# The first half of k over the hardware queues: a fused attention and feed-forward kernel

## The chip, the cores and the metric

The kernel runs on one core of a Trainium2 chip. The metric is the device time of one execution in microseconds (us). The core has five engines that run side by side, each taking its own instructions in order: TensorE (PE in the profile; PEld is its weight load), VectorE (DVE), ScalarE (ACT), GpSimd (POOL) and SyncE (SP). Transfers between the device's memory and the core's memory go through 16 DMA engines. They are issued on queues: GpSimd's is a software queue (q0 in the profile) whose transfers may change the number type on the way; SyncE's (q1) and ScalarE's (q10) are hardware queues, on which this kernel moves data in its own type.

## The reference

q, k and v have the shape [8, 8, 576, 64] (batch, heads, sequence, head size), all float32. Attention runs in a window of 32 positions to each side; its result is put together over the heads and goes through two matrix products with a smooth unit between them. The constants are filled in here:

```python
scores = matmul(q, k.transpose(0, 1, 3, 2)) / sqrt(64)
scores = where(abs(pos[:, None] - pos[None, :]) <= 32, scores, -1e9)
attn = softmax(scores)                       # over the last axis
x = matmul(attn, v).transpose(0, 2, 1, 3).reshape(4608, 512)
h = x @ w_in                                 # [4608, 2048]
g = where(h >= 1, h, where(h <= -1, 0, (h + 1) ** 2 / 4))
out = g @ w_out                              # [4608, 512]
```

## The kernel before

The matrix work is done in bfloat16, with sums in float32. The tokens are taken in blocks of 256 (`TB`); a block's first product is made in eight steps of 256 columns (L504, into the tile `hp`), each followed by the unit on ScalarE and VectorE (`rr`, `mx`, `gT`, L508 to L516), and the second product (L433, L444, L460) follows in pieces laid between later steps. The loop at L482 counts these steps as `a`. The attention of the eight batches is cut into pieces (scores, sums) that a hand-written table places at steps of that loop. All engines follow the order in which the program writes their instructions (`manual_schedule`); nothing is reordered.

The loop can't begin before the first block of attention is there, so the kernel opens with a stage of its own, which is where the change lies. Four heads of a batch lie in one half of the partitions and four in the other. The first batch's q and k come in two halves of heads, and each half in two transfers (`load_half`, L80; `h` picks the half of the partitions that is read from). In the first half:

- q is loaded in float32 into `q32` by SyncE (h = 0) and ScalarE (h = 1), 128 rows of 2304 B each. It is turned into bfloat16 on chip by `cast` (L338): VectorE converts five of nine parts of each row (`cut` = 5), ScalarE the other four, into `qb`.
- k is loaded by GpSimd's software queue in two transfers that convert to bfloat16 on the way, into `kh`. They are GpSimd's first two DMA issues. Behind them on GpSimd stand an `affine_select` (L131, from which VectorE makes the identity and the band masks), four loads of v (L134), four pieces of w_in, and then the second half of q and k and more weights (L149 to L157).

Q and k are then transposed on TensorE by `tpose` (L169), which writes into PSUM in two parts, of five and four column groups. Where its source is a tile that `cast` made, it transposes 128x128 at once (L189, nine matmuls for q). Where its source came straight from a transfer, it takes the two 64-column halves one after the other (L187, eighteen matmuls). The two parts are copied out of PSUM into `qT` and `kT` (L190), the first by ScalarE and the second by VectorE.

The order of the opening (L346 to L370) is: eleven filler matmuls on TensorE that use no input (`keep_warm`, L336, tile `z`), the cast of q, q's transposes, q's two copies, k's transposes, three fillers, k's two copies, then the first scores. Scores begin with matmuls that put the band mask into PSUM (L206), then the products of kT and qT (L227), then the exponential on ScalarE (L235, tile `pt`). After more fillers come the sums over v and over ones (L293), logarithm and exponential on ScalarE for the reciprocal (L299, L300), and the scaled result into `xT` on VectorE (L305). The first `hp` reads that `xT`.

Of the kernel before, what the change touches and what calls it, by code (L numbers as in the profile page):

```python
# [7 lines left out]
FP = mybir.dt.float32  # L8
# [6 lines left out]
def kernel(  # L15
# [19 lines left out]
    nc = tc.nc  # L35
    B, H, S, D = q.shape
# [40 lines left out]
    qn, kn, vn = {}, {}, {}  # L77
    HD = (slice(0, 64), slice(64, 128))

    def load_half(half, t, h, eng=None, x=None):  # L80

        src, dst, nm = ((q, qn, "qh"), (k, kn, "kh"))[t]
        if (0, half) not in dst:
            dst[0, half] = early.tile([128, 2, S], BF, name=nm, tag=nm, bufs=2) if x is None else x
        (eng or nc.gpsimd).dma_start(out=dst[0, half][:, h], in_=src[0].rearrange(
            "(h y) (l p j) d -> h l p y (j d)", h=2, l=2, p=32)[h][half])
# [29 lines left out]
                            in_=moe_w_out.rearrange("(ko ki) f -> ki ko f", ki=128)[:, k0:k1, 256 * c:256 * c + 256])  # L116

    early = ctx.enter_context(tc.tile_pool(name="early", bufs=1))
    q32 = early.tile([128, 2, S], FP, name="q32")
    for h in range(2):  # L120
        load_half(0, 0, h, (nc.sync, nc.scalar)[h], q32)
    for h in range(2):
        load_half(0, 1, h)
    A.preload_act_table_set("natural_log_exp_and_others")
    warm = const.tile([128, 512], BF, name="warm")
    V.memset(warm, 0.0)
# [35 lines left out]
    def qkT(b, t):  # L162
        if t == 0:
            return qTs[b % 3][:, PAD:]
        if b not in kT:
            kT[b] = ktp.tile([128, NY * S], BF, name="kT")
        return kT[b]

    def tpose(b, n, t, copy, ps):  # L169


        half, part = divmod(n, 2)
        j0, j1 = ((0, 5), (5, 9))[part]
        if b:
            src = qn[b] if t == 0 else kn[b]
            src = [src[:, half + 2 * h] for h in range(2)]
            dst = qkT(b, t).rearrange("d (y e p j) -> d y e p j", y=2, e=2, j=9)[:, half, :, :, j0:j1]
            like = "d j (e p) -> d e p j"
        else:
            src = (qn, kn)[t][b, half]  # L180
            src = src if src.shape[1] == 9 else [src[:, h] for h in range(2)]
            dst = qkT(b, t).rearrange("d (y l p j) -> d l y p j", l=2, p=32, j=9)[:, half, :, :, j0:j1]
            like = "d j (p y) -> d y p j"
        for j in range(j0, j1):
            if isinstance(src, list):
                for h in range(2):
                    nc.tensor.transpose(ps[HD[h], j - j0], src[h][:, D * j:D * j + D], ident)  # L187
            else:
                nc.tensor.transpose(ps[:, j - j0], src[:, j], ident)  # L189
        return lambda: copy(dst, ps[:, :j1 - j0].rearrange(like, p=64 if b else 32))  # L190
# [20 lines left out]
    def scores(b, ys, pars, cs, eng, pool=ps_s, w=128):  # L211

        if b not in pt:
            pt[b] = ptp.tile([128, 2, 2, 2, 512], BF, name="pt")
        ps = two_banks(pool)
        n = 0
        if eng is None:
            cols = (ys[1] - ys[0]) * (pars[1] - pars[0]) * (cs[1] - cs[0])
            add_mask([ps[:, h] for h in range(2)], cols, w)
        for y1 in range(*ys):  # L220
            for par in range(*pars):
                for c2 in range(*cs):
                    c = 2 * c2 + par
                    for a in range(2):
                        for h in range(2):
                            s0 = S * (y1 + 2 * a) + 64 * c
                            nc.tensor.matmul(ps[HD[a], h, w * n:w * n + w], kT[b][HD[h], s0:s0 + 64],  # L227
                                             qTs[b % 3][HD[h], PAD + s0 - 32:PAD + s0 - 32 + w],
                                             start=eng is not None, stop=True, skip_group_check=True)
                    n += 1  # L230
        p = pt[b][:, :, ys[0]:ys[1], pars[0]:pars[1], 128 * cs[0]:128 * cs[1] - 128 + w]
        m = 2 if n > cs[1] - cs[0] else 1
        p = p[:, :, ys[0] - ys[0]] if ys[1] - ys[0] == 1 else p[:, :, :, 0]
        like = "p h (y j) -> p h y j"
        A.activation(p, ps[:, :, :w * n].rearrange(like, y=m), AF.Exp, scale=D ** -0.5)  # L235
        mask(eng, p, mask4[:, :256 * n].rearrange("p (h j) -> p h j", h=2).rearrange(like, y=m))
# [81 lines left out]
    def tp1(pool):  # L318
        if pool is ps_h:
            return pool.tile([128, 8, 128], BF, name="tp", tag="hp")  # L320
        return pool.tile([128, 2, 8, 128], BF, name="tp", tag="bb")[:, 0]
# [10 lines left out]
    def keep_warm(n, pool, tag):  # L332

        z = pool.tile([128, 512], FP, name="z", tag=tag)
        for _ in range(n):
            nc.tensor.matmul(z, warm[:, :128], warm, start=True, stop=True)  # L336

    def cast(x, nm, cut):  # L338

        y = early.tile([128, 9, 2, D], BF, name=nm)  # L340
        o, i = y.rearrange("p j h d -> p h j d"), x.rearrange("p h (j d) -> p h j d", d=D)
        V.tensor_copy(o[:, :, :cut], i[:, :, :cut])
        A.copy(o[:, :, cut:], i[:, :, cut:])
        return y.rearrange("p j h d -> p j (h d)")

    with tc.tile_pool(name="ps_p", bufs=1, space=bass.MemoryType.PSUM) as ps_p:  # L346
        keep_warm(11, ps_h, "hp")

        V.memset(qkT(0, 0).rearrange("d (y s) -> d y s", y=NY)[:, :, S // 2:352], 0.0)
        for b in range(LONG):  # L350
            V.memset(qkT(b, 0).rearrange("d (y s) -> d y s", y=NY)[:, :, S - PAD:], 0.0)
        V.memset(qkT(0, 1).rearrange("d (y s) -> d y s", y=NY)[:, :, S // 2:320], 0.0)
        qn[0, 0] = cast(q32, "qb", 5)
        qq = [tpose(0, n, 0, (A.copy, V.tensor_copy)[n], tp1(ps_h)) for n in range(2)]
        for x in qq:
            x()
        kk = [tpose(0, n, 1, (A.copy, V.tensor_copy)[n], tp1((ps_n, ps_p)[n])) for n in range(2)]
        keep_warm(3, ps_h, "hp")
        for x in kk:
            x()  # L360
        scores(0, (0, 1), (0, 2), (0, 2), None)
        scores(0, (0, 2), (0, 1), (2, 3), None, ps_n, 32)
        scores(0, (1, 2), (0, 2), (0, 2), None, ps_p)
        keep_warm(4, ps_h, "hp")
        e0 = sums(0, 0, 0, TB)
        keep_warm(2, ps_h, "hp")
        e1 = sums(0, 1, 0, TB, ps_p)
        keep_warm(7, ps_h, "hp")
        e0()
        e1()  # L370
# [111 lines left out]
    for a in range(NF * NB + NF):  # L482
        t, f = divmod(a, NF)
# [70 lines left out]
```

## Time and profile before

| what | value |
| --- | --- |
| time, median of 4 runs | 308.59 us (308.56 to 308.73) |
| the profiled execution: time | 308.56 us |
| its span, first to last instruction | 306.8 us |
| TensorE busy | 300.4 us (98% of the span) |
| VectorE busy | 241.8 us (79%) |
| ScalarE busy | 192.3 us (63%) |
| GpSimd busy | 76.8 us (25%) |
| granted TensorE clock | 1.00 throughout |
| first q issues, SyncE and ScalarE | 0.74 us, 4.4 and 3.8 us to landing |
| first k issues, GpSimd | from 1.26 us, 1.26 us for both |
| first v issues, GpSimd | from 2.94 us, 3.44 us for the four |
| first scores on TensorE | 8.62 us |
| first exponential on ScalarE | 9.08 us |
| first xT on VectorE | 12.57 us |

The times in the lower part are positions in the span of the profiled execution. "Time to landing" runs from the issue to the moment at which the transfer's semaphore says that all of it is there. A busy engine isn't always a useful one: the fillers count as busy time of TensorE.

### The profile page before, as it was taken

To read this page: it belongs to the slowest core of one execution; us is meant where nothing else is said; L and a number is where in the kernel's file an instruction comes from. 1 tells how busy PE (TensorE), PEld (TensorE's weight loads), DVE (VectorE), ACT (ScalarE), POOL (GpSimd) and SP (SyncE) were. 2 spreads that over 40 slices of the span, in tenths; PEclk is the share of its full clock that TensorE was granted. 3 is DMA by queue.
4 is the path that set the end of the run, shared out by engine and by line. 5 is a ranking of instruction groups with operands and counts; after the bars stand their busy time and mean duration, and the time that the engine had idled before them with its cause. 6 is when DMAs were issued, how large, how long until landed. Compare 5 with 4: busy or idle time off the path is not lost.

```text
span 306.8 us, 8495 instructions
## 1 busy us (share of the span) xinstructions
PE 300.4 (98%) x3650; PEld 206.8 (67%) x3650; DVE 241.8 (79%) x376; ACT 192.3 (63%) x320; POOL 76.8 (25%) x91
## 2 busy tenths in 40 slices
PE   8989999999999999999999999999999999999995
PEld 3567878876666666666666666666666666666654
DVE  3278568888888888889888888889888888888760
ACT  3688786738856667666656666566676666554431
POOL 8898461037008205500550004600000000000000
PEclk9999999999999999999999999999999999999999
DMA  9999999999999998996899157990811011010111
GB/s 150 184 196 198 180 201 153 174 152 158 131 200 86 168 190 97 164 105 142 105 167 140 34 107 100 170 139 17 177 50 36 34 36 36 35 36 34 59 45 68
DMA packets 137157, 35.70 MB, mean 116 GB/s; under 512 B 122144, under 2 KB 132896, under 8 KB 137120
## 3 DMA queue, kind: packets, MB, share of 16 engines
q0 software_dynamic: 102960, 18.06, 84.0%
q1 hardware_dynamic: 34016, 16.81, 25.5%
q8 instruction: 28, 0.46, 0.6%
q10 hardware_dynamic: 144, 0.29, 0.4%
q14 instruction: 9, 0.07, 0.1%
HBM read 36.70 MB, written 9.44 MB: 150 GB/s over the span
## 4 chain that ended last, share of the span: by engine, by line
PE 93%; ACT 3%; DVE 2%; issue 1%; ACTq 0%
PE hp L504 39%; PE op L444 36%; PE bb L293 6%; PE op L460 4%; PE bb L227 2%; PE z L336 2%; PE op L433 1%; PE tp L187 1%; ACT pt L235 1%; DVE xT L305 1%; ACT rc L300 1%; ACT lr L299 1%; DVE mx L515 0%; ACT rr L508 0%; PE tp L189 0%
## 5 line engine op out<-in xcount | busy, mean ns | idle before, releaser
L504 PE MATMUL hp<-xT,w_in 128*128 128x256 bf16 x1152 | 149.6, 273 | 1.6 <-DMA w_in<-in_moe_w_in_dram 0.7
L508 ACT ACTIVATE rr<-hp 128x512 f32<-128x512 f32 x144 | 85.6, 594 | 88.1 <-PE hp L504 88.1
L504 PEld LDWEIGHTS <-w_in 128*128 128x128 bf16 x1152 | 112.0, 98 | 41.3 <-issue 1.6
L444 PE MATMUL op<-w_out,gT 128*128 128x512 bf16 x496 | 127.0, 380 | 0.0
L515 DVE TENSOR_TENSOR mx<-hp,rr 128x512 f32<-128x512 f32 x137 | 94.5, 690 | 30.9 <-ACT rr L508 28.8
L516 DVE SCALAR_TENSOR_TENSOR gT<-rr,mx 128x512 bf16<-128x512 f32 x137 | 95.2, 695 | 4.7
L444 PEld LDWEIGHTS <-gT 128*128 128x128 bf16 x496 | 46.1, 98 | 34.8
L98 POOL DMA_DIRECT2D qn<-in_q_dram x12 | 14.6, 1224 | 111.5 <-DMA kT<-kn 107.7
L235 ACT ACTIVATE pt<-bb 128x1024 bf16<-128x1024 f32 (+1 forms) x33 | 32.7, 1001 | 4.8 <-PE bb L227 3.5
L305 DVE TENSOR_TENSOR xT<-bb,rc 128x512 bf16<-128x512 f32 (+1 forms) x32 | 21.0, 658 | 9.9 <-ACT rc L300 9.3
L106 POOL DMA_DIRECT2D vn<-in_v_dram x32 | 27.5, 902 | 3.7 <-DMA w_out<-in_moe_w_out_dram 3.7
L300 ACT ACTIVATE rc<-lr 128x512 f32<-128x512 f32 (+2 forms) x40 | 23.5, 587 | 1.3
L449 ACT COPY osb<-op 128x512 f32<-128x512 f32 x31 | 18.0, 582 | 8.7 <-PE op L444 8.3
L299 ACT ACTIVATE lr<-bb 128x512 f32<-128x512 f32 (+2 forms) x40 | 22.1, 552 | 0.2
L201 DVE TENSOR_TENSOR pt<-pt,mask 128x1024 bf16<-128x1024 bf16 (+1 forms) x33 | 20.3, 614 | 0.5 <-ACT pt L235 0.5
L293 PE MATMUL bb<-pt,ones 64*64 64x256 bf16 (+3 forms) x352 | 19.6, 256 | 0.1
L293 PE MATMUL bb<-pt,vn 64*64 64x128 bf16 (+3 forms) x712 | 18.4, 204 | 0.0
L293 PEld LDWEIGHTS <-vn 64*64 64x64 bf16 x712 | 16.7, 107 | 0.1
L460 PE MATMUL op<-w_out,gT 128*128 128x256 bf16 x128 | 16.5, 273 | 0.0
L293 PEld LDWEIGHTS <-ones 64*64 64x64 bf16 x352 | 10.2, 105 | 8.9 <-issue 8.9
L98 POOL DMA_DIRECT2D kn<-in_k_dram x12 | 14.6, 1235 | 0.5 <-issue 0.2
L460 PEld LDWEIGHTS <-gT 128*128 128x128 bf16 x128 | 12.0, 98 | 1.9
(59 smaller groups left out, 115.8 us busy)
## 6 DMA issues: line engine op xcount, KB each, us to landing
out_dram<-osb SPq DMA_DIRECT2D x35, 256.0 KB, 2.4
vn<-in_v_dram POOLq DMA_DIRECT2D x32, 144.0 KB, 10.3
qn<-in_q_dram POOLq DMA_DIRECT2D x12, 288.0 KB, 7.3
kn<-in_k_dram POOLq DMA_DIRECT2D x12, 288.0 KB, 9.3
w_in<-in_moe_w_in_dram POOLq DMA_DIRECT2D x12, 128.0 KB, 5.9
w_out<-in_moe_w_out_dram POOLq DMA_DIRECT2D x3, 512.0 KB, 15.6
kh<-in_k_dram POOLq DMA_DIRECT2D x4, 144.0 KB, 5.3
qn<-in_q_dram POOLq DMA_DIRECT2D x1, 576.0 KB, 9.8
```

The costliest lines, as they stand in the source:

```text
L98: nc.gpsimd.dma_start(out=x[:, :, h], in_=src[b, NY * h:NY * h + NY].rearrange("y s d -> (y s) d") .rearrange("(u p) d -> p u d", p=128))
L106: nc.gpsimd.dma_start(out=vn[b][64 * a:64 * a + 64, :, h], in_=v[b, y:y + 2].rearrange("y s d -> (y s) d") .rearrange("(c r) d -> r c d", ...
L235: A.activation(p, ps[:, :, :w * n].rearrange(like, y=m), AF.Exp, scale=D ** -0.5)
L293: nc.tensor.matmul(bb[HD[h], a, o + c0:o + c1], ones[HD[a]] if c is None else vn[b][HD[a], c, h], p(a, h), start=n == 0, stop=True, skip_g ...
L299: A.activation(lr[:, :, :D0], bb[:, :, D0:2 * D0], AF.Ln)
L300: A.activation(rc[:, :, :D0], lr[:, :, :D0], AF.Exp, scale=-1.0)
L444: nc.tensor.matmul(o, gT[tt // 2][:, j, 128 * (tt % 2):128 * (tt % 2) + 128], w_out[:, j], start=not done, stop=len(done) == 2 * NF - 1, s ...
L460: nc.tensor.matmul(o[:, tt], gT[p][:, j, 128 * tt:128 * tt + 128], w_out[:, j, 256 * half:256 * half + 256], start=not done, stop=len(done ...
L504: nc.tensor.matmul(hp[:, j], w_in[:, kk, 256 * f + 128 * j:256 * f + 128 * j + 128], xT[:, kk, r0:r0 + TB], start=n == 0, stop=n == 3)
L508: A.activation(rr, hp, AF.Relu, scale=0.5, bias=0.5)
L515: V.tensor_max(mx, hp, rr)
L516: V.scalar_tensor_tensor(g, rr, 1.0, mx, op0=ALU.min, op1=ALU.mult)
```

## The change

Both transfers of the first half of k go the way that q's go: in float32 over SyncE's and ScalarE's queues, each behind q's on the same queue, into a new tile `k32`. A second `cast` turns `k32` into the bfloat16 tile `kb`, and stands right behind q's cast in the program, so ahead of the copies of q's transposes on both VectorE and ScalarE. GpSimd issues neither of them any more; its first issue is the load of v behind `affine_select`. The transposes of this half of k take the path of a cast tile (L189). The second half of q and k is loaded as before.

```diff
     early = ctx.enter_context(tc.tile_pool(name="early", bufs=1))
-    q32 = early.tile([128, 2, S], FP, name="q32")
-    for h in range(2):
-        load_half(0, 0, h, (nc.sync, nc.scalar)[h], q32)
-    for h in range(2):
-        load_half(0, 1, h)
+    q32, k32 = [early.tile([128, 2, S], FP, name=nm) for nm in ("q32", "k32")]
+    for t, x in enumerate((q32, k32)):
+        for h in range(2):
+            load_half(0, t, h, (nc.sync, nc.scalar)[h], x)
     A.preload_act_table_set("natural_log_exp_and_others")
...
         qn[0, 0] = cast(q32, "qb", 5)
+        kn[0, 0] = cast(k32, "kb", 5)
         qq = [tpose(0, n, 0, (A.copy, V.tensor_copy)[n], tp1(ps_h)) for n in range(2)]
```

## The prediction

> **What bounds the kernel now.** I read the busy table by stage first, then the waits of TensorE, then the chain of waits over the opening, then the timeline and the DMA packets of the microseconds that the change touches.
>
> Busy time by stage (stage in us: length, PE, PEld, DVE, ACT, POOL busy, clock, DMA share, GB/s):
>
> ```profile
> 5.91:8.62 2.71, 2.71 (x35) 1.79 (x36) 1.38 (x2) 1.51 (x2) 2.71 (x5) 1.00 2.75 151
> 8.62:14.60 5.98, 5.56 (x123) 3.00 (x120) 1.38 (x2) 4.56 (x7) 4.85 (x9) 1.00 1.67 188
> 14.60:28.40 13.80, 12.59 (x242) 9.75 (x242) 10.74 (x17) 11.03 (x21) 12.99 (x18) 1.00 1.39 197
> 28.40:300.00 271.60, 271.40 (x3215) 187.95 (x3215) 226.05 (x342) 172.04 (x287) 51.44 (x51) 1.00 1.09 111
> ```
>
> From 28.4 us on TensorE is busy 271.40 of 271.60 us, so nothing loaded earlier can shorten that part: what the opening gains or loses passes one to one into the end. The change acts in the opening alone, and there the chain of waits (start, length, what) says who sets the pace:
>
> ```profile
> 6.07 0.98 PE tp L189 x9
> 7.05 0.65 PE tp L187 x18
> 7.70 0.75 PE z L336 x3
> 8.45 0.34 PE bb L206 x4
> 8.79 0.24 PE bb L227 x16
> ...
> 10.54 0.72 PE bb L293 x24
> 11.26 0.02 issue
> 11.28 0.60 ACT lr L299
> ...
> ```
>
> The transposes of q (L189) and of k (L187), three filler matmuls and the first scores stand in one row on TensorE; from the first exponential on ScalarE carries the chain to 13.84, then VectorE's xT, written from 13.86. The timeline (start, length, engine, line, operation, idle before) shows what each waits for:
>
> ```profile
> 5.20 0.62 ACT L343 CAST qb<-q 128x512 bf16<-128x512 f32 x1 [2.51 <-DMA q<-in_q_dram]
> 5.21 0.64 DVE L342 CAST qb<-q 128x640 bf16<-128x640 f32 x1 [1.15 <-DMA q<-in_q_dram]
> 5.91 1.14 PE L189 MATMUL tp<-ident,qb 128*128 128x128 bf16 x9
> 6.98 0.72 PE L187 MATMUL tp<-ident,kh 128*64 128x128 bf16 x18
> 7.09 0.73 DVE L190 COPY qT<-tp 128x512 bf16<-128x512 bf16 x1 [1.24 <-PE tp L189]
> 7.74 0.73 DVE L190 COPY kT<-tp 128x512 bf16<-128x512 bf16 x1
> 8.62 0.41 PE L227 MATMUL bb<-qT,kT 64*64 64x128 bf16 x16
> 9.08 1.02 ACT L235 ACTIVATE pt<-bb 128x1024 bf16<-128x1024 f32 x1 [0.80 <-PE bb L227]
> ```
>
> k's transposes follow q's without a wait for k: today k is in time. The first scores (L227) at 8.62 are what I follow, since everything up to 14.6 hangs on them.
>
> **The change part by part.**
>
> *k's transposes.* As a cast tile k is transposed by nine 128x128 matmuls (the path of L189) in place of eighteen 128x64 ones that run in pairs. The chain gives 0.98 for the nine of q and 0.65 for the eighteen: +0.33 us; by starts in the timeline nine take 6.98-5.91 = 1.07, with fill, so I take 0.96 (9 x 107 ns) as the step from k's first transpose to the fillers. Fillers 0.75 and mask matmuls 0.24 stay. So the first scores start 0.96+0.75+0.24 = 1.95 after k's first transpose: with that transpose at 6.98 they are at 8.93, +0.31. VectorE agrees: q's second copy starts 1.18 after q's first transpose and k's would too, plus 0.72, which makes 1.90.
>
> *The casts.* One more cast on VectorE (0.64 us, L342) and one on ScalarE (0.62, L343). Had k landed by 5.8 they would lie in the idle time before 6.66 and 7.09 and cost nothing. The time from cast start to first transpose is 5.91-5.20 = 0.71. So k's first transpose is at 6.98, or 0.71 after k's casts can start, whichever is later; the casts must start by 6.27 to be free. This is the wait that the change adds. Behind it on VectorE and ScalarE stand the copies of qT, then of kT, on TensorE three fillers, the mask matmuls and the scores; ScalarE's exponential waits for them all. q's copies, put off behind the cast, end 0.64+0.73 after the cast starts, before kT can be copied, and add nothing of their own.
>
> *When k lands.* SyncE and ScalarE each issue q at 0.74 (0.65 and 0.64 long) and now k at 1.39 in the same queues. Neither issue is on the path: ScalarE's table load moves from 1.41 to about 2.05 and ends at 3.3, under its 2.51 us idle before the cast at 5.20; SyncE issues nothing else before 34.9. The packets, from the DMA view of three windows (2 to 3.5, 3.5 to 4.5 and 54.25 to 55.25 us, in this order):
>
> ```profile
> DMA packets 100, 0.23 MB, mean 152 GB/s; under 512 B 1, under 2 KB 1, under 8 KB 100
> ...
> DMA packets 197, 0.37 MB, mean 372 GB/s; under 512 B 25, under 2 KB 46, under 8 KB 197
> ...
> q1 hardware_dynamic: 194, 0.20, 83.0%
> q0 software_dynamic: 290, 0.04, 66.1%
> ```
>
> q and k are 4 x 0.295 = 1.18 MB. Up to 3.5 us 0.23 MB are through; 0.95 MB at the 372 GB/s of the next window take 2.55 us, so k's last packet goes at 6.05 if nothing shares the engines. But GpSimd, without its two k issues, sends v sooner. Its affine_select can run when VectorE's step is set (1.41), so v's first issue starts near 1.88, not 2.94. k's first software packets came some 2.8 us after their issue began (21 of queue 0 fall in the window 3.5 to 4.5), which puts v's near 4.7, when 0.95-1.2x0.372 = 0.50 MB of q and k are still to come. What small software packets do to a hardware transfer the third window shows: an output store (queue 1) beside input loads in 128-byte pieces kept 83% of the engines' time, and moved 0.20 MB in that us, in smaller packets. 83% of 372 is 0.31 MB/us: 0.50 MB take 1.6 us, to 6.33; the bare 0.20 MB/us would take 2.5 us, to 7.2. I take 0.31, since q's and k's rows of 2304 B are the longer pieces that the 372 belong to. From the last packets of q (12 of queue 1 after 4.5, so about 4.75) to the casts at 5.20 is 0.45. So k's casts start at 6.05+0.45 = 6.5 at best by this view, 6.78 by my choice, 7.65 by the other end. I keep 6.27 (free) as the lower bound, because 372 is a mean in which the software queue was already sharing.
>
> With 6.78: first transpose of k 7.49, first scores 9.44, +0.82. Ends: +0.31 and (7.65+0.71+1.95-8.62) +1.69.
>
> *q itself* now shares with k where it shared with kh from 4 us on. Its casts could be late by up to 0.2 us or early by as much. Early gains nothing: eleven fillers hold TensorE to 5.91. Late is hidden below 0.3 us, since k's first transpose is already at 7.49 against 7.05 for the end of q's. If k were in time, it would show in full.
>
> *TensorE's pause* of 0.4 us between q's and k's transposes: in this trace it pauses 0.72 us at 17.5 and the granted clock stays 1.00, so no slower clock is charged.
>
> *v and the weights earlier.* ScalarE's three exponentials run from 9.08 for 2.11, to 11.19, and its next step starts at 11.28 behind the sums: the sums may win back 0.09 at most, and only if v held them. I credit it. TensorE's wait of 0.72 us for w_in at 17.5 may go, but the chain there runs through VectorE's copies of qT and kT (18.25 to 19.61) to the scores at 19.67, and gains nothing. The half-1 tiles qh and kh follow on GpSimd's queue, some 0.5 us sooner at most; nobody waited for them.
>
> Sum: +0.82-0.09 = **+0.73**, between +0.2 and +1.6. The profiled execution took 308.56 us (span 306.8), 0.03 under the median 308.59. It makes 309.3.
>
> [...] The trace: both q issues start at 0.74 and last 0.65 and 0.64, but in the window 2 to 3.5 us ScalarE's queue (q10) had 96 packets and SyncE's (q1) 4, so SyncE's data began about 1 us later. [...]
>
> **Rivals.**
> - *k in time.* The packets keep the 372 GB/s or better, and the casts hide: only the transposes' +0.31, less 0.09: 308.56+0.22 = 308.8. For: kh and q shared the engines too and both were in time. Against: k would have to be castable by 6.27, before the 6.5 that the bandwidth gives.
> - *Queues in turn.* If the starts are spaced by 1 us (2.2, 3.2, 4.2, 5.2) and each transfer takes SyncE's 1.55 us (3.2 to 4.75), k's last packet goes near 6.8, casts at 7.25, first scores 9.91: +1.29-0.09, 309.8.
> - *The early queue pays (not slower).* If the sums wait for v (first sums 0.72 us in the chain, the second group's rows 0.63 from start to end: 0.09 to gain) and the 0.72 wait for w_in at 17.5 is on the path after all, with k in time: 308.56+0.31-0.09-0.72 = 308.1. It decides from the point where VectorE's kT copy (to 19.61) isn't the last before the scores at 19.67. Against: the chain goes through just that copy.
>
> **How the numbers follow.** What a measurement here can tell from no change is about 0.2%, 0.62 us. Forecast 0.55 (own range 308.9 to 309.9), k in time 0.19, queues in turn 0.16, early queue 0.10. Above 309.2 lie three quarters of the forecast (0.42) and the queues in turn (0.16): slower 0.58. Within: the rest of the forecast (0.13), k in time (0.19) and 0.04 of the last: 0.36. Faster: 0.06. The range goes from 308.7, under k in time, to 310.2, the sum's upper end; about 0.15 is left out, most of it the early queue.
>
> **What would show it.** k's cast with idle time before it, released by k's DMA, starting near 6.8; nine transposes of kb; the first scores near 9.4, the first exponential near 9.9 and the first xT 0.7 later than 12.57; from 28 us on nothing but a shift. Wrong would be: no wait before k's cast (then 308.8), a cast after 7.2, or a span that moves by another amount than the first exponential does.

## The result, and the profile after

The changed kernel takes 309.31 us (median of 52 runs, 308.86 to 313.42) against 308.8 for the kernel before, measured beside it (73 runs). The ratio of the two is 1.0026, with a 95% interval of 1.0015 to 1.0036. The forecast was 309.3. The profiled execution took 309.52 us, its span 307.7 (306.8 before). A ratio leaves out executions over 1.5% above the fastest of the same kernel: below that is one, of 313.8 us, under "v issued later".

The timeline of the opening (start, length, engine, line, operation, idle before; lines from L124 to L353 of the kernel before sit one lower here, later ones keep their number):

```profile
5.74 0.68 PE L188 MATMUL tp<-ident,qb 128*128 128x128 bf16 x9 [0.22 <-DVE qb L341]
6.72 0.62 ACT L342 CAST kb<-k 128x512 bf16<-128x512 f32 x1 [1.03 <-DMA k<-in_k_dram]
6.74 0.49 DVE L341 CAST kb<-k 128x640 bf16<-128x640 f32 x1 [1.06 <-DMA k<-in_k_dram]
7.15 0.72 DVE L189 COPY qT<-tp 128x512 bf16<-128x512 bf16 x1
7.29 0.68 PE L188 MATMUL tp<-ident,kb 128*128 128x128 bf16 x9 [0.88 <-DVE kb L341]
8.01 0.72 DVE L189 COPY kT<-tp 128x512 bf16<-128x512 bf16 x1
9.03 0.39 PE L226 MATMUL bb<-qT,kT 64*64 64x128 bf16 x16
...
12.82 0.69 DVE L304 TENSOR_TENSOR xT<-bb,rc 128x512 bf16<-128x512 f32 x1 [4.10 <-ACT rc L299]
```

There is the new wait: both engines stand idle for about a microsecond until k has landed, q's copies stand behind the casts, and TensorE waits 0.88 us for the cast. The first scores come at 9.03 in place of 8.62, the first xT at 12.82 in place of 12.57: +0.25 us. The span grew by 0.9. The rest shows in the waits of TensorE (in total, times, longest):

```profile
PE hp L504 <- DMA w_in<-in_moe_w_in_dram: 1.8, 2, 1.2
PE tp L188 <- DVE kb L341: 0.9, 1, 0.9
```

and in the chain of waits up to 24 us, which this execution's end hangs on:

```profile
1.84 6.27 DMA vn<-in_v_dram
8.11 0.28 issue
8.39 6.79 DMA qh<-in_q_dram
15.18 0.28 issue
15.47 0.60 POOL w_in L110
16.07 7.49 DMA w_in<-in_moe_w_in_dram
23.56 0.14 issue
23.69 0.38 PE hp L504 x2
```

TensorE waits 1.23 us for a piece of w_in. This chain stays on GpSimd's queue throughout: v, the second half of q, then w_in, each issue held until an older transfer has landed. The first output copy of the main loop (L449) stands at 72.47 us against 71.38: +1.1. Was that wait the change's doing, or this execution's? The next section's second run answers.

The packets by queue in four windows, 2 to 3.5, 3.5 to 4.5, 4.5 to 5.5 and 5.5 to 6.5 us (packets, MB, share of 16 engines):

```profile
q10 hardware_dynamic: 95, 0.22, 79.4%
...
q1 hardware_dynamic: 130, 0.29, 76.8%
q10 hardware_dynamic: 57, 0.09, 24.7%
...
q10 hardware_dynamic: 136, 0.28, 70.8%
q1 hardware_dynamic: 64, 0.12, 32.3%
...
q0 software_dynamic: 669, 0.09, 133.7%
q1 hardware_dynamic: 94, 0.18, 46.4%
```

In this trace the four transfers go largely in turn: ScalarE's q, SyncE's q, ScalarE's k, SyncE's k. The software queue, with v issued at 1.84, moves nothing before 5.5.

### The profile page after: what moved, and what is told of

Read it like the earlier page. It is cut to its first block, busy times and chain, and to the rows that moved or that the text cites. A ratio compares the mean times of both kernels' runs of the same rounds, so it can differ in the third digit from the quotient of the medians.

```text
span 307.7 us, 8483 instructions
## 1 busy us (share of the span) xinstructions
PE 299.2 (97%) x3641; PEld 206.3 (67%) x3641; DVE 242.5 (79%) x377; ACT 192.9 (63%) x321; POOL 75.8 (25%) x89
## 4 chain that ended last, share of the span: by engine, by line
PE 90%; DMA 7%; ACT 1%; DVE 0%; issue 0%; POOL 0%; ACTq 0%
PE hp L504 39%; PE op L444 36%; PE bb L292 6%; PE op L460 4%; DMA w_in<-in_moe_w_in_dram 2%; DMA qh<-in_q_dram 2%; PE bb L226 2%; DMA vn<-in_v_dram 2%; PE op L433 1%; PE tp L186 1%; ACT pt L234 1%; DVE gT L513 0%; ACT mx L512 0%; PE bb L251 0%; ACT rr L508 0%
## 5 line engine op out<-in xcount | busy, mean ns | idle before, releaser
L449 ACT COPY osb<-op 128x512 f32<-128x512 f32 x31 | 18.0, 582 | 8.7 <-PE op L444 8.3
```

## The experiments

Each is an edit of the changed kernel unless it says otherwise, and each ratio is against the kernel before, run beside it on the same chip. Where two runs differ by a number or a line, one diff stands for both; the comments in the diffs are not in the code.

**Both kernels again.** No edit.

> The kernel before, unchanged. It tells what one profiled execution varies by: where the granted clock begins (7.1 us in the first trace), when the first scores start (8.62) and how long TensorE waits for w_in between 17 and 24 us (0.72). If the 1.2 us wait for w_in at 23.7 in the changed kernel is chance, a trace of this one may show it too; if it comes from the change, it shows 0.8 or less again. Ratio 1.000 within 0.001.

> The changed kernel, unchanged. Theory 1 (the late cast of k sets the start): k's cast starts at 6.6 to 6.9 again, first scores at 9.0 to 9.3, and the span is 0.3 to 0.9 over the other one's. Theory 2 (the weights come late because the transfers are reordered): TensorE waits for w_in at about 23.7 for 1 us or more again. If that wait is gone and the time stays 0.5 or more over, theory 1 carries it; if it comes and goes, it is chance.

Measured: the kernel before 1.0003 (0.9990 to 1.0016), the changed one 1.0012 (1.0004 to 1.0021). The kernel before, seen again:

```profile
5.90 0.72 PE L189 MATMUL tp<-ident,qb 128*128 128x128 bf16 x9
6.55 0.24 PE L187 MATMUL tp<-ident,kh 128*64 128x128 bf16 x1
7.03 0.69 PE L187 MATMUL tp<-ident,kh 128*64 128x128 bf16 x17 [0.23 <-DMA kh<-in_k_dram]
8.64 0.41 PE L227 MATMUL bb<-qT,kT 64*64 64x128 bf16 x16
```

q's nine transposes take 0.72 us here and took 1.14 in the first trace. So k, which seemed in time, holds TensorE for 0.23 us even in the kernel before: it had no slack, and the slow transposes of q had hidden that. The changed kernel again:

```profile
6.86 0.67 DVE L341 CAST kb<-k 128x640 bf16<-128x640 f32 x1 [1.18 <-DMA k<-in_k_dram]
7.59 0.68 PE L188 MATMUL tp<-ident,kb 128*128 128x128 bf16 x9 [1.17 <-DVE kb L341]
9.17 0.42 PE L226 MATMUL bb<-qT,kT 64*64 64x128 bf16 x16
...
18.50 1.03 PE L504 MATMUL hp<-xT,w_in 128*128 128x256 bf16 x8 [0.62 <-DMA w_in<-in_moe_w_in_dram]
```

The wait for k is there again, a little longer; the wait of 1.23 us at 23.7 is not. The first output copy stands at 71.79, +0.4 over the first trace of the kernel before, which is what the first xT lost (12.99 against 12.57). So of these two traces the late k is the part in common, and the wait of 1.23 us for w_in comes and goes. The span of this execution is 307.0 against 306.8 and 306.9 for the two traces of the kernel before.

**k's wait taken away.** In this run, k's cast reads q's tile: the first half of the first batch's scores is made of q in place of k. The transfers stay.

```diff
-        kn[0, 0] = cast(k32, "kb", 5)
+        kn[0, 0] = cast(q32, "kb", 5)
```

> k's cast reads q's tile, which is there, so the kernel computes its first half of the first batch's scores from q in place of k; all four transfers stay. Theory 1: k's cast stands right behind q's, near 5.7, the first scores come 0.5 to 0.9 earlier than in the changed kernel (8.2 to 8.5), and the time falls by 0.3 to 0.8, to that of the kernel before or below. Theory 2: the first scores come as early, but the wait for w_in grows by as much, and the time stays within 0.2 of the changed kernel's.

Measured: 1.0002 (0.9990 to 1.0013), median 308.89 against 308.66. The start of TensorE's work on scores and sums:

```profile
8.01 0.39 PE L226 MATMUL bb<-qT,kT 64*64 64x128 bf16 x16
...
10.52 0.28 PE L292 MATMUL bb<-pt,vn 64*64 64x96 bf16 x8 [0.33 <-DMA vn<-in_v_dram]
...
12.36 0.69 DVE L304 TENSOR_TENSOR xT<-bb,rc 128x512 bf16<-128x512 f32 x1 [4.56 <-ACT rc L299]
```

Scores start a microsecond sooner than in the changed kernel and 0.6 sooner than in the kernel before. The time can't be told from that of the kernel before. That it is below the changed kernel's, seen again on the same chip (1.0012), is likely but not shown, since the intervals overlap; what the trace shows is that without the wait the loss in the opening is gone. It also shows why nothing is gained: the sums now wait for v, which the earlier issue was to bring, so that the first xT is only 0.21 sooner than in the kernel before (12.36 against 12.57), and by the first output copy (71.51 against 71.38 and 71.45) that is gone too.

**v issued later.** Two and then five fills of an unused tile on GpSimd put v's first issue at 3.10 and, in the second run, at 5.16 us in place of 1.84.

```diff
+    idle = early.tile([128, 640], FP, name="idle")
+    for _ in range(2):          # range(5) in the second run
+        P.memset(idle, 0.0)
     for n in range(4):
         load_v(0, n)
```

> The changed kernel with two fills of an unused tile on GpSimd ahead of the loads of v, some 1 us in all, which puts v's issues back to where they stood before. If the DMA engines are full with q and k until about 6 us, v's data come at the same time and the time is that of the changed kernel within 0.2 us; nothing was gained by v's earlier issue. If the earlier issue is worth something, the time is 0.3 to 1 us longer.

> The changed kernel with five fills of an unused tile ahead of v's loads, which puts v's first issue near 5.0 us in place of 1.84. It brackets v's slack. v's first packets came near 5.7 in every trace, whether it was issued at 1.84, 2.94 or 3.10. Issued at 5.0 they come near 7, v lands more than 1 us later, the first sums wait for v, and the time rises by 0.7 to 1.5 over the changed kernel. If v had slack of its own, the time stays.

Measured: 1.0008 (0.9994 to 1.0022) and 1.0040 (1.0025 to 1.0056). Issued 1.26 us later, v costs nothing that can be measured. In that trace the window 4.1 to 5.5 us holds 143 packets of SyncE's queue, 131 of ScalarE's and none of the software queue, and the next microsecond 954 of the software queue (669 in the changed kernel, the first of them at 5.79). Only in the second run do the first sums wait for v, 0.85 us. So the earlier place on GpSimd's queue bought nothing. That the two hardware queues kept v out is likely, not shown: in the changed kernel they took 53.9% and 48.5% of the engines' time between 4.1 and 5.5 us. Two of the twelve executions of the first run had a mean clock of 0.994 and 0.989; what that means comes under the fillers.

**The transposes.** k's cast tile is laid out like the loaded one, so that eighteen small transposes take the place of nine.

```diff
-        kn[0, 0] = cast(k32, "kb", 5)
+        kn[0, 0] = cast18(k32, "kb", 5)     # same two casts, into [128, 2, S]
```

> The changed kernel with k's cast tile laid out like the loaded one, so that its transposes are eighteen 128x64 matmuls again. The prediction charged 0.31 us for the nine full ones (0.96 against 0.65). The later traces have the nine of a cast tile in 0.68, at full clock. If the charge is right, the step from k's first transpose to the first scores falls from about 1.7 to 1.4 and the time by 0.3; if the row of 1.14 was one of a slow clock, step and time stay within 0.1 us of the changed kernel's.

```profile
7.86 0.49 DVE L340 CAST kb<-k 128x640 bf16<-128x640 f32 x1 [2.18 <-DMA k<-in_k_dram]
8.40 0.69 PE L186 MATMUL tp<-ident,kb 128*64 128x128 bf16 x18 [1.56 <-DVE kb L340]
10.15 0.39 PE L226 MATMUL bb<-qT,kT 64*64 64x128 bf16 x16
```

Ratio 1.0005 (0.9991 to 1.0019). Eighteen take 0.69 us and nine 0.68; from k's first transpose to the first scores it is 1.75 us, against 1.74 and 1.58 in the two traces of the changed kernel. The 0.31 that I charged for the nine isn't there. The same lines show how far k's arrival wanders: 7.86 here, with the same four transfers. In this trace SyncE's part of k took 6.3 us from issue to landing and ScalarE's 4.4, where the first trace of the changed kernel has 5.2 and 4.4.

**The order on the two engines.** k's cast behind q's copies.

```diff
-        kn[0, 0] = cast(k32, "kb", 5)
         qq = [tpose(0, n, 0, (A.copy, V.tensor_copy)[n], tp1(ps_h)) for n in range(2)]
         for x in qq:
             x()
+        kn[0, 0] = cast(k32, "kb", 5)
```

> The changed kernel with k's cast written behind the two copies of q's transposes. The prediction put the loss on k's arrival, not on the copies that queue behind the cast. Then the copies of q move into the idle time, VectorE's cast of k starts only after its copy (near 7.2 in place of 6.7 to 6.9), the first scores come 0.2 to 0.4 later, and the time is 0.1 to 0.4 longer. If the queue behind the cast were the loss, the first scores would come 0.3 or more sooner.

Measured: 1.0001 (0.9990 to 1.0012). The casts started at 7.14, with no idle time before them, and the first scores at 9.29, as foreseen, but the time didn't rise. In this trace k landed about when q's copies were done, so the order hardly mattered. That it is better than the changed kernel isn't shown: the intervals overlap.

**All on one hardware queue.**

```diff
-            load_half(0, t, h, (nc.sync, nc.scalar)[h], x)
+            load_half(0, t, h, nc.sync, x)
```

> All four transfers of q and k are issued by SyncE. If the hardware queues are served in turn by whatever feeds the engines, as the four blocks of packets in the changed kernel's trace look, the blocks follow each other as before, q's cast starts near 5.0 and k's at 6.4 to 6.9, and the time is that of the changed kernel within 0.3 us. If two queues side by side carry more than one, k's cast starts 0.5 us later or more and the time rises as much.

Measured: 1.0137 (1.0116 to 1.0158). The cast of k, and the packets of the window 4 to 5.5 us:

```profile
10.07 0.49 DVE L341 CAST kb<-k 128x640 bf16<-128x640 f32 x1 [4.39 <-DMA k<-in_k_dram]
```

```profile
q0 software_dynamic: 529, 0.07, 70.2%
q1 hardware_dynamic: 115, 0.23, 51.0%
```

A miss for "turns only". q's cast starts at 5.01, as in the changed kernel (5.09 and 4.90), but then v does move before 5.5, and k, which moves beside it, is castable only at 10.07. With both hardware queues loaded, the same window held none of v, and 0.58 MB went over them in place of 0.23.

Not all of the lost time is k's. The granted clock was halved for two stages, the first of which begins 1.1 us before the wait's end (length, PE, PEld, DVE, ACT, POOL, clock, DMA share, GB/s):

```profile
6.10:9.40 3.30, 0.53 (x9) 0.36 (x7) 0.00 (x0) 0.00 (x0) 1.73 (x3) 1.00 2.06 196
9.50:12.90 3.40, 2.28 (x12) 1.25 (x12) 1.85 (x3) 2.03 (x3) 1.38 (x3) 0.50 2.28 167
12.90:16.30 3.40, 3.07 (x56) 1.79 (x56) 0.00 (x0) 2.11 (x3) 2.82 (x6) 0.50 1.20 179
```

All four executions had a mean clock of 0.989 to 0.994. How much each part costs wasn't separated.

**The fillers.** One filler in place of three ahead of the first scores, in the changed kernel and, as a control, in the kernel before.

```diff
-        keep_warm(3, ps_h, "hp")
+        keep_warm(1, ps_h, "hp")
```

> The changed kernel with one filler matmul in place of three between k's transposes and the first scores. In its trace the copy of kT ends at 8.73 and the first scores start at 9.03, behind fillers and mask matmuls. If fillers hold the scores there, they start within 0.1 us of the copy's end and the time falls by 0.1 to 0.3 us; the loss against the kernel before shrinks by that and is not gone, as k's landing stays. If the copy holds them, nothing changes. A third way is that the pause lowers the clock, and matmuls after it are slower.

> The control: the kernel before with one filler in place of three at the same place. There the copy of kT ends at 8.47 and the scores start at 8.62, so at most 0.15 us is to be had: time 0 to 0.15 below before, and below the changed kernel with one filler if k's landing is what separates the two.

Measured: the kernel before 0.9997 (0.9986 to 1.0008), the changed one 1.0034 (1.0010 to 1.0059), with five of ten runs between 311.0 and 311.8. Its trace is one of those five:

```profile
8.27 0.49 DVE L341 CAST kb<-k 128x640 bf16<-128x640 f32 x1 [2.58 <-DMA k<-in_k_dram]
8.82 1.14 PE L188 MATMUL tp<-ident,kb 128*128 128x128 bf16 x9 [2.40 <-DVE kb L341]
```

Busy time by stage (length, PE, PEld, DVE, ACT, POOL, clock, DMA share, GB/s):

```profile
5.40:8.70 3.30, 1.01 (x11) 0.50 (x9) 0.71 (x3) 0.47 (x2) 2.43 (x4) 1.00 2.59 174
8.80:12.10 3.30, 3.28 (x57) 2.17 (x59) 1.31 (x2) 2.03 (x4) 1.98 (x4) 0.50 1.86 170
12.20:15.50 3.30, 3.09 (x76) 1.73 (x70) 0.22 (x1) 2.91 (x6) 2.83 (x6) 1.00 1.26 202
```

k came late, TensorE was busy for 1.01 of 3.30 us, and from 8.8 to 12.1 us the granted clock was 0.50, with 1.00 up to 8.7 and from 12.2; the nine transposes then took 1.14 us again. This pause lies ahead of the place of the edit. So the trace doesn't show that the missing fillers made such executions more frequent; it may be the chip, as each group of runs had another.

One such window, 3.4 us as the middle between 3.3 and 3.5, takes the mean clock of an execution to 1 - 0.5 x 3.4/309 = 0.9945, two to 0.989. Of the changed kernel's own 53 executions (the timed ones and the profiled one) eight had a mean clock of 0.989 to 0.995, and they took 310.7 to 313.4 us; the other 45 took at most 309.99. Of the kernel before, 90 timed executions beside the experiments had none below 0.998. The twelve of the changed kernel run again had none either, and neither had those with k's wait taken away or with the cast behind the copies; of the twelve with eighteen transposes one had. No trace was taken of one of those eight, so that they are the same thing rests on their clock and their time.

**Filling the wait.** Three fillers moved from behind k's transposes to ahead of them, or six added there.

```diff
+        keep_warm(3, ps_h, "hp")            # 6 in the second run
         kk = [tpose(0, n, 1, (A.copy, V.tensor_copy)[n], tp1((ps_n, ps_p)[n])) for n in range(2)]
-        keep_warm(3, ps_h, "hp")            # kept in the second run
```

> The changed kernel with its three fillers moved from behind k's transposes to ahead of them, into TensorE's wait for k's cast. In executions where k lands late the wait was seen to halve the granted clock for 3.4 us. Theory: late k makes both the shift and the halved clock. Then the wait shrinks by 0.6 us, executions with a mean clock under 0.996 become rarer than 8 in 53 (0 or 1 of 12), the first scores start about 1.5 us after k's first transpose, and the time is within 0.3 us of the changed kernel's usual 309.2, not below the kernel before. If the pause has no part in it, as many executions as before lose 2 to 4 us.

> The changed kernel with six more fillers (some 1.3 us) between q's and k's transposes, its three kept. If the halved clock comes from the pause, no execution has a mean clock under 0.996. The price: the fillers end near 7.7 and hold k's transposes in executions where k is early (cast done by 7.2), 0.3 to 0.5 us, and cost nothing where k is late. Times lie at 309.2 to 309.8 in a narrower band. If the slow clock has another cause, executions over 310.5 us stay.

Measured: 1.0100 (1.0060 to 1.0139) and 1.0092 (1.0064 to 1.0120), both far worse than foreseen. The first one's fillers and their wait:

```profile
8.41 1.44 PE L335 MATMUL z<-warm 128*128 128x512 bf16 x3 [1.99 <-ACT qT L189]
9.64 1.17 PE L188 MATMUL tp<-ident,kb 128*128 128x128 bf16 x9
```

```profile
8.10:11.40 3.30, 2.97 (x16) 1.44 (x15) 0.68 (x2) 1.00 (x2) 1.92 (x4) 0.50 2.57 159
```

The fillers write into the buffers that q's transposes had just used, so they wait for ScalarE's copy of qT, and that copy stands behind the cast of k, which waits for k. The edit made the pause longer (1.99 us), and going by the mean clock (0.989 to 0.995) five of six runs of the first had a halved clock and three of six of the second. The others, at full clock, took 310.1 to 311.1 us, so the longer wait costs time by itself. It doesn't test the remedy, but it shows the halved clock at such a pause again, and what it costs that q's copies queue behind the cast as soon as somebody waits for them. Fillers into another buffer weren't tried.

No version beat the kernel before: the best ratios, 0.9997 and 1.0001, can't be told from 1.

## Why the prediction was right, and where it wasn't

The mechanism of the forecast holds: k's casts wait for k, the first scores come later, and the kernel gets slower by a few tenths of a microsecond. That the number is met to 0.01 is luck. The median moved by 0.51, from 308.8 to 309.31, where +0.73 on 308.56 was forecast, and the terms were off in both directions.

- *k's casts at 6.78.* Measured 6.72 and 6.86. The way to it was wrong in one place: v was to share the engines with k from 4.7 us, and moved nothing before 5.5. In the first trace the four transfers went in turn instead, as the second rival had it, but k's two in about 1 us each where the rival took 1.55. k's two issues, started within 0.05 us of each other, lasted 0.62 (ScalarE) and 0.83 us (SyncE) in the first trace and 0.88 and 0.58 in the second, and each time the longer one landed second: from issue to landing they took 4.4 and 5.2 us in the first trace, 5.4 and 4.7 in the second. q's two issues are equal (0.64 and 0.66 us in the first trace), and landed 0.8 us apart. What makes the order, no run here shows.
- *From casts to transposes, 0.71.* Measured 0.57 (6.72 to 7.29) and 0.73 (6.86 to 7.59).
- *Nine transposes for eighteen, +0.31.* This is the term that failed: 0.69 against 0.68, and no change in the step to the scores. I had taken 107 ns each from a row of 1.14 us, without seeing that TensorE ran slowly there. In the chain of the kernel before, the eleven fillers ahead of it took 0.44 us each (`1.19 4.88 PE z L336 x11`) and the three behind k's transposes 0.25 (`7.70 0.75 PE z L336 x3`). The clock column doesn't tell: it shows 1.00 for the stage 5.91 to 8.62, in which the row of 1.14 lies, and "1.00 throughout" in the table ahead was read from it. The durations show the slow start: 1.14 and 0.72 for the same nine in two traces of the kernel before, 0.68 in the changed one. So do the starts of the matmuls, 107 ns apart in the row of 1.14 and 56 in the row of 0.68. The clock's record begins only at 7.08 us of the span, behind that row, and at 4.82 in the changed kernel's trace, ahead of both its rows of nine. Why a trace starts slowly, no run here shows.
- *First scores +0.82.* Measured +0.41 and +0.55, less than forecast mainly because of that term.
- *Sums, -0.09.* About -0.15: the first exponential came 0.40 later, the first xT only 0.25.
- *"Today k is in time."* It landed at the last moment; two of three traces of the kernel before, one of them with the fillers cut to one, show TensorE waiting for it (0.23 us at 7.03, 0.18 at 6.94). A k that lands no earlier and has a cast still ahead of it loses by the cast.
- *"No slower clock is charged."* Wrong in the tail. I had a pause of 0.4 us between q's and k's transposes, counted with the slow row of q; it measured 0.88 and 1.17, and 2.40 where the clock fell. The mean of the 45 executions at full clock, 309.31, is 0.38 us over the mean of the kernel before, 308.93; the eight others lift the mean of the 52 timed ones to 309.72, another 0.41. So about half of the mean loss comes with those eight. How much of it is the clock's and how much a later k's isn't separated, since the trace with one filler has both. My 0.73 came out near the ratio's 0.8 (0.0026 x 308.8) by luck: the transposes charged for nothing and the tail left out were of a size.
- *"One to one into the end."* Only roughly. I had named a span that moves by another amount than the first exponential as a sign of being wrong, and it shows: the exponential came 0.40 and 0.55 later in the two traces, the spans grew by 0.9 and 0.2. In the first the wait for w_in came on top. The mean of +0.38 at full clock lies near the first xT's +0.25 and +0.42.
- *Rivals.* "k in time" fell: VectorE and ScalarE waited for k in every trace with its cast in the place that the change gave it. "The early queue pays" fell with v issued later at no cost, and with k's wait removed for no gain beyond the kernel before.

## What to carry to other kernels

A transfer moved to another queue only helps if it lands sooner where it is used, its cast included; add up the bytes that must land by then and divide by what the engines move, before asking which queue issues them. Before a row of the opening prices a step, look at the fillers beside it to see whether TensorE ran at full speed. And where the order of instructions is fixed, a wait put on an engine is inherited by all that stand behind it, down to a filler that only wants a buffer back.

## What the runs showed of the hardware

- v's first packets, on the software queue, came at 5.79 us in the changed kernel, issued at 1.84, and at 5.65 in the kernel before, issued at 2.94. Issued at 3.10, with both hardware queues in use, none came between 4.1 and 5.5 us and 954 in the next microsecond; issued at 5.16, v kept the first sums waiting for 0.85 us. With one hardware queue in use, 529 packets of the software queue came between 4 and 5.5 us, and k was castable only at 10.07. Why, no run shows.
- Pauses of TensorE of 2.40 us (with 1.01 us of work in a stage of 3.30) and 1.99 us each ended in a stage of 3.30 us at a granted clock of 0.50, and one of 3.99 us (all on one queue) in 6.8 us of it. Behind one of 2.09 us (six fillers added) the nine transposes took 1.17 us, and the mean clock of that execution was 0.995. A pause of 1.56 us (eighteen transposes) left the mean clock of its execution at 1.00.
- The same four loads made k castable anywhere from 6.45 to 8.27 us across the traces. In the latest one k's two transfers took 6.4 us (SyncE) and 6.8 (ScalarE) from issue to landing, against 5.2 and 4.4 in the first trace of the changed kernel, and v's first 7.3 against 6.3. With v issued at 5.16, k was castable at 6.97. What moves it, no run shows.
